# One attention burst per tile, and the state product in a place of its own, in a fused attention, feed-forward and routed-experts kernel

## Chip, core and metric

The kernel runs on one core of a Trainium2 chip. The metric is the device time of one execution in microseconds (us); lower is better. The kernel before took 869.97 to 872.79 us in three timed runs, with a median of 872.28.

## What is computed

Three layers follow each other. The first is a linear-attention recurrence over 768 steps for 4 batches, 8 heads and head size 48; the second a gated feed-forward over the 3072 resulting tokens (width 384, inner width 1536); the third sends each token to one of 8 experts.

```python
# attention, per batch and head
cur = (u * k_t) outer v_t
y_t = r_t @ (state + cur)
state = w[:, None] * state + k_t outer v_t
# feed-forward
x = (silu(x @ w_gate) * (x @ w_val)) @ w_out
# experts: e = argmax(x @ gate); scaled by softmax and a sigmoid gate
out = gate * (relu(x @ w1[e]) @ w2[e])
```

## The kernel before

Attention works on 24 tiles of 128 tokens (NT), one batch each; tile i belongs to batch i % 4 and to the sequence chunk i // 4, of which there are 6 (TPB). Inside a tile the recurrence is written as matrix products. Four kinds of them run on TensorE for a tile:

- the **scores** (`a_scores`, L363): 16 fp32 matmul instructions with 64 rows each, so two of them share the array by rows. They go to banks 6 and 7;
- the **state product** (L378, inside `a_out_mm`): what the state of earlier chunks gives to this tile's output; 8 full-array fp32 instructions;
- the **values** (L387, `a_out_mm`): the masked scores times v; 16 instructions of 48 columns, so two share the array by columns. They add to the state product in the same bank (6);
- the **state matmuls** (L424, `a_state_mm`): k times v, 16 instructions of 48 columns, to bank 7. Tiles of the last chunk (20 to 23) have none.

Around them, VectorE scales k and r by decay tables (`a_scale`, L316), reduces the bonus (L334), copies the scores through a mask into the tile `at` (`a_mask`, L368) and adds the new state (`a_state_up`, L440). GpSimd makes the bonus (L324, L325), a diagonal in `at` (`a_diag`, L343), the scaled keys (`a_keys`, L352) and the decay of the state (`a_decay`, L445). `a_out_ev` takes a tile's output out of PSUM: ScalarE copies a rounded part (L407), VectorE the remainder (L408), first for three column groups into `xT`, then for the fourth into `stage`. After the third tile of a block six DMAs on SP (L412) move `stage` into `xT`. There is one buffer for `krT` (k and r of a tile) and one for `at`.

The feed-forward works on blocks of 3 tiles (BT), 8 blocks (NBLK), 384 tokens each. For each of 12 slices f of the inner width `b_block` issues a gate product (9 matmuls, L475), a down product of slice f - 2 (9 matmuls, L494), a value product (9 matmuls, L475), and `b_act`: Silu on ScalarE (L483), the multiply on VectorE (L484), a rounded cast on ScalarE (L486) and the remainder (L487, on VectorE from block 1 on). Weights and activations are f32r pairs, so a product is three passes over three chunks. Gate and value products go to a ring of banks that `next_gv` hands out: 3, 4 and 5 from block 1 on, 3 and 4 in block 0, where bank 5 is scratch for the weight conversion. Down products gather in banks 0 to 2; ScalarE empties them in slice 1 of the next block (L505).

The order is written out by hand: while block b runs, the attention of the three tiles of block b + 1 is put into 24 slots. Slot 2f comes behind the gate product of slice f, slot 2f + 1 behind its value product and its `b_act`. `a_place` fills them for a tile from slot `first` (0, 8 or 16) on: load, scale, diagonal, then keys, scores and mask, then `a_out` (state product, values, state matmuls, decay, output), the loads of the next tile, and last the state add. For the third tile of a block, scores and `a_out` come one slot earlier (`e`), so behind a gate product. The routing of the block before (`c_units`, two small bf16 products into bank 6), a scan of the weights (L265 on GpSimd) in blocks 2 to 5 and the clearing of a DRAM buffer by 32 DMAs in block 1 have slots too. Block 7 carries no attention; then the experts follow.

Each engine takes its instructions in the order in which they are issued; a wait holds all behind it on that engine.

Of the kernel before, what the change touches and what calls it, by code (L numbers as in the profile page):

```python
# [21 lines left out]
NB, NH, S, HD = 4, 8, 768, 48  # L22
NTOK = NB * S
NT = NTOK // P
TPB = S // P
# [7 lines left out]
BT = 3  # L33
BN = BT * P
# [17 lines left out]
def kernel(  # L52
# [12 lines left out]
    pe, act, dve, pool, sp = nc.tensor, nc.scalar, nc.vector, nc.gpsimd, nc.sync  # L65
# [227 lines left out]
    def a_load_kr(i):  # L293
        n = a_tile(i)
        if i < 3:
            t = kr3[i]
            att[i] = {"k": (t[:, 0], t[:, 2]), "r": t[:, 1]}
            sp.dma_start(out=t[0:HD, 0:2], in_=krT_d[n, 0])
            sp.dma_start(out=t[64 : 64 + HD, 2], in_=krT_d[n, 1, :, 0])
            sp.dma_start(out=t[64 : 64 + HD, 1], in_=krT_d[n, 1, :, 1])  # L300
        else:
            att[i].update({"k": krT[:, 0], "r": krT[:, 1]})
            for j in range(2):
                sp.dma_start(out=krT[64 * j : 64 * j + HD], in_=krT_d[n, j])

    def a_load(i):
        if i < 3:
            rkv = spare[NF - 4 - i][:, 0 : 3 * DM].rearrange("s (a c) -> s a c", a=3)
        else:
            rkv = apool.tile([P, 3, DM], F32, tag="rkv", name="rkv", bufs=2)  # L310
        sp.dma_start(out=rkv, in_=rkv_d[a_tile(i)])
        att.setdefault(i, {}).update({"rn": rkv[:, 0], "kn": rkv[:, 1], "vn": rkv[:, 2]})

    def a_scale(i, parts=(0, 1)):
        if i >= 3:
            dve.tensor_tensor(out=krT, in0=krT, in1=WT, op=ALU.mult)  # L316
        elif 0 in parts:
            dve.tensor_tensor(out=kr3[i][:, 0:2], in0=kr3[i][:, 0:2], in1=WT, op=ALU.mult)
        if i < 3 and 1 in parts:
            dve.tensor_tensor(out=kr3[i][:, 2], in0=kr3[i][:, 2], in1=WkT, op=ALU.mult)  # L320

    def a_bonus(i):
        t = att[i]
        pool.tensor_tensor(out=t["rn"], in0=t["rn"], in1=ub, op=ALU.mult)  # L324
        pool.tensor_tensor(out=t["rn"], in0=t["rn"], in1=t["kn"], op=ALU.mult)  # L325

    def a_diag(i, on_act):
        t = att[i]
        a = apool.tile([P, NH], F32, tag="a", name="a", bufs=2)
        if i < 3:  # L330
            at = spare[NF - 4 - i][:, 3 * DM : 3 * DM + 8 * P].rearrange("s (j p t) -> s j p t", j=2, p=4)
        else:
            at = apool.tile([P, 2, 4, P], F32, tag="at", name="at", bufs=1)
        dve.tensor_reduce(  # L334
            out=a.rearrange("s (j p) -> s p j", j=2), in_=t["rn"].rearrange("s (p j d) -> s p j d", p=4, j=2),
            op=ALU.add, axis=AX.X,
        )
        af = at.rearrange("s j p t -> s (j p) t")
        if on_act:
            for h in range(NH):  # L340
                act.mul(out=af[:, h], in_=ident, mul=a[:, h : h + 1])
        else:
            pool.tensor_tensor(out=af, in0=bc(ident, 1, [P, NH, P]), in1=bc(a, 2, [P, NH, P]), op=ALU.mult)  # L343
        t["at"] = at

    def a_keys(i):
        if i // NB < TPB - 1:
            k = kp
            if i < 3:
                k = kr3[i][:, 0].rearrange("s p t -> s (p t)").rearrange("s (h d) -> s h d", h=NH)  # L350
            att[i]["kp"] = k
            pool.tensor_tensor(  # L352
                out=k[:, :, 0:HD], in0=att[i]["kn"].rearrange("s (h d) -> s h d", h=NH),
                in1=Wk.rearrange("s (h d) -> s h d", h=NH), op=ALU.mult,
            )

    def a_scores(i, b0=6):
        for p in range(4):
            for j in range(2):
                q = slice(64 * j, 64 * j + 64)  # L360
                k, r = att[i]["k"], att[i]["r"]
                k, r = (k[j][:, p], r[:, p]) if i < 3 else (k[q, p], r[q, p])
                pe.matmul(bank[b0 + j][:, p * P : (p + 1) * P], k, r, start=True, stop=True)  # L363

    def a_mask(i, b0=6):
        at = att[i]["at"]
        for j in range(2):
            dve.copy_predicated(  # L368
                at[:, j], bc(mask, 1, [P, 4, P]), bank[b0 + j].rearrange("s (p t) -> s p t", p=4)
            )  # L370

    def a_out_mm(i, b=6, pairs=(3, 0, 1, 2)):
        vn, at, r = att[i]["vn"], att[i]["at"], att[i]["r"]
        c, S0 = i // NB, Sst[i % NB]
        y = bank[b].rearrange("s (p t) -> s p t", p=4)
        if c > 0:
            for p in pairs:
                pe.matmul(  # L378
                    y[:, p], S0[:, p].rearrange("s j e -> s (j e)"), r[:, p, :],
                    start=(p == pairs[0]), stop=False, skip_group_check=True,  # L380
                )
        for p in pairs:
            if i < BT and p < 3:
                pe.matmul(y[:, p], shf[:, p], y3[i], start=True, stop=False)
            for j in range(2):
                h = 2 * p + j
                pe.matmul(  # L387
                    y[64 * j : 64 * j + HD, p], vn[:, h * HD : (h + 1) * HD], at[:, j, p, :],
                    start=(c == 0 and (i >= BT or p == 3)), stop=True, skip_group_check=c > 0,
                )  # L390
            if i < BT and p == 3:
                for j in range(2):
                    q = slice(64 * j, 64 * j + HD)
                    act.copy(out=y3[i][q], in_=y[q, 3])
# [3 lines left out]
    def a_out_ev(i, b=6):  # L398
        y = bank[b].rearrange("s (p t) -> s p t", p=4)
        blk, t = divmod(i, BT)  # L400
        if t == 0:
            xT[blk] = bpool.tile([P, 2, KC, BN], F32R, tag="xT", name="xT", bufs=2)
            if blk > 0:
                stage[blk] = bpool.tile([P, 2, BN], F32R, tag="stage", name="stage", bufs=1)
        o = slice(t * P, (t + 1) * P)
        for x, n in ((xT[blk][:, :, :, o], y[:, 0:KC]),) + (((stage[blk][:, :, o], y[:, KC]),) if blk > 0 else ()):
            act.copy(out=x[:, 0], in_=n)  # L407
            dve.tensor_tensor(out=x[:, 1], in0=n, in1=x[:, 0].bitcast(F32), op=ALU.subtract)  # L408
        if t == BT - 1 and blk > 0:
            for cc in range(KC):  # L410
                for j in range(2):
                    sp.dma_start(  # L412
                        out=xT[blk].bitcast(F32)[64 * j + HD : 64 * j + 64, :, cc, :],
                        in_=stage[blk].bitcast(F32)[64 * j + 16 * cc : 64 * j + 16 * cc + 16],
                    )
# [29 lines left out]
            pool.tensor_tensor(out=sv, in0=sv, in1=bc(pw[:, 0, :, 7], 2, [P, 4, P]), op=ALU.mult)  # L445

    def a_out(i):
        a_out_mm(i)
        a_state_mm(i, 7)
        a_decay(i)  # L450
        a_out_ev(i)

    def a_state(i, b):
        a_state_mm(i, b)
# [2 lines left out]
    hT = {}  # L457
    gvn = [0]

    def next_gv(blk):  # L460
        b = bank[3 + gvn[0] % (3 if blk else 2)]
        gvn[0] += 1
        return b[:, 0:BN]

    PASSES = ((0, 0), (0, 1), (1, 0))

    def b_up(blk, f, *gvs):
        x = xT[blk]
        ps = [next_gv(blk) for _ in gvs]
        first = blk == 0 and f < 2  # L470
        order = [(c, gv, n) for c in range(KC) for gv in range(len(gvs)) for n in range(3)]
        for c, i, n in sorted(order, key=lambda u: first and u[2] == 2):
            wl, xl = PASSES[n]
            o = (gvs[i] * KC + c) * P
            pe.matmul(  # L475
                ps[i], W[f][:, wl, o : o + P], x[:, xl, c, :],
                start=(c == 0 and n == 0), stop=(c == KC - 1 and n == 2),
            )
        return ps
# [112 lines left out]
        return [r1, lambda: c_prefix(st["r"]), r2]  # L592

    def a_place(slots, i, first):
        def load():
            if i + 1 < NT:
                a_load(i + 1)

        def load_kr():
            if i + 1 < NT:  # L600
                a_load_kr(i + 1)

        def bonus():
            if i + 1 < NT:
                a_bonus(i + 1)

        def diag():
            a_diag(i, BT < i < 2 * BT)

        def scores():  # L610
            a_scores(i)
            a_mask(i)

        slots[first].append(load)
        slots[first + (i == BT)].append(lambda: a_scale(i))
        slots[first + 1].append(diag)
        e = 1 if i % BT == BT - 1 else 0
        slots[first + 3 - e] += [lambda: a_keys(i), scores]
        slots[first + 5 - e] += [lambda: a_out(i), load_kr, bonus]
        slots[first + 6].append(lambda: a_state_up(i, 7))  # L620

    raws = {}

# [527 lines left out]
```

## Time and profile before

| | |
|---|---|
| three timed runs | 872.28, 869.97, 872.79 us |
| profiled execution | 870.72 us, its span 869.0 us |
| TensorE busy | 827.0 us, 95% of the span |
| VectorE, ScalarE, GpSimd busy | 460.4, 272.0, 270.5 us |
| gate and value products, L475 | 1728 matmuls, 331.5 us |
| down products, L494 | 864 matmuls, 176.6 us |
| scores, values, state product, state matmuls from SBUF tiles (L363, L387, L378, L424) | 26.3, 22.7, 21.1, 9.0 us |

The span runs from the first to the last instruction; the rest of the execution's time lies around it. Matmuls overlap in the array, so the busy time of a group says less than the distance from the start of one group to the start of the next. That distance is what the text uses for TensorE.

### The profile page before, as it was taken

The numbers are of one execution on the slowest core, as the hardware profiler recorded it, in microseconds if no ns is written. First come the engines' busy times: TensorE is split into PE (matmuls) and PEld (weight loads), VectorE is DVE, ScalarE is ACT, GpSimd is POOL, SyncE is SP. The second block draws the span as 40 slices with busy tenths as digits, with TensorE's granted clock in tenths as the row PEclk, the third lists the DMA queues.
The fourth block names the chain that finished last, engine by engine and source line by source line (L and its number), as shares of the span: only waits on it lengthen the run. The fifth ranks groups of instructions, "written<-read, shape, count | busy, mean of one in ns | idle before, by whom it ended". The sixth has DMA issues, their size and how long they took to land.

```text
span 869.0 us, 13844 instructions
## 1 busy us (share of the span) xinstructions
PE 827.0 (95%) x5427; PEld 797.1 (92%) x5427; DVE 460.4 (53%) x945; ACT 272.0 (31%) x590; POOL 270.5 (31%) x241
## 2 busy tenths in 40 slices
PE   3878889999999999999999999999989999999996
PEld 3667789999999999999999999999989999999996
DVE  7797762454465455465455444234555655565541
ACT  2324342122212211221212221323444444444432
POOL 6655645232344335335245112010110210121022
PEclk9879989999999999999999999999999999999998
DMA  8615426734234322322323211410484443544200
GB/s 256 218 72 192 145 82 153 205 111 123 100 100 131 108 103 68 139 81 95 118 88 129 60 46 47 160 50 1 162 311 148 140 163 113 163 136 166 83 26 35
DMA packets 29769, 104.90 MB, mean 121 GB/s; under 512 B 5175, under 2 KB 14193, under 8 KB 26624
## 3 DMA queue, kind: packets, MB, share of 16 engines
q1 hardware_dynamic: 26368, 94.37, 33.8%
q0 software_dynamic: 3328, 9.56, 2.9%
q8 instruction: 45, 0.74, 0.4%
q14 instruction: 28, 0.23, 0.1%
HBM read 85.84 MB, written 16.41 MB: 118 GB/s over the span
## 4 chain that ended last, share of the span: by engine, by line
PE 83%; DVE 7%; issue 5%; DMA 2%; ACT 1%; POOL 1%; POOLq 0%; SPq 0%; DVEq 0%
PE bank L475 32%; PE bank L494 18%; PE bank L691 11%; PE bank L708 11%; PE bank L363 3%; PE bank L387 3%; PE bank L378 2%; DVE bank L215 2%; DVE bank L214 2%; DMA spare<-in_rkv_dram 2%; DVE cv L216 2%; PE bank L656 1%; PE bank L722 1%; PE bank L424 1%; POOL out_dram L730 0%
## 5 line engine op out<-in xcount | busy, mean ns | idle before, releaser
L475 PE MATMUL bank<-xT,W 128*128 128x384 f32 x1728 | 331.5, 342 | 0.2 <-DVE xT L408 0.2
L475 PEld LDWEIGHTS bank<-xT,W 128*128 128x128 f32 x1728 | 305.0, 189 | 3.2 <-DVE xT L408 0.5
L494 PE MATMUL bank<-W,h 128*128 128x400 f32 x864 | 176.6, 349 | 0.0
L494 PEld LDWEIGHTS bank<-W,h 128*128 128x128 f32 x864 | 156.8, 190 | 1.9 <-issue 0.6
L486 ACT CAST h<-s 128x384 fp32r<-128x384 f32 x96 | 49.2, 512 | 323.5 <-DVE s L484 323.5
L484 DVE TENSOR_TENSOR s<-s,bank 128x384 f32<-128x384 f32 x96 | 53.1, 553 | 174.0 <-PE bank L475 148.6
L708 PE MATMUL bank<-hd,wf 128*128 128x416 f32 (+1 forms) x576 | 113.8, 344 | 0.0
L708 PEld LDWEIGHTS bank<-hd,wf 128*128 128x128 f32 x576 | 104.3, 188 | 0.7 <-DVE hd L695 0.2
L730 POOL DMA_INDIRECT out_dram<-yo,ix x32 | 34.6, 1081 | 206.3 <-DVE yo L726 179.3
L487 DVE TENSOR_TENSOR h<-s,h 128x384 fp32r<-128x384 f32 x84 | 60.5, 720 | 48.6 <-ACT h L486 48.6
L695 DVE SCALAR_TENSOR_TENSOR hd<-bank,hd 128x416 fp32r<-128x416 f32 (+1 forms) x64 | 36.7, 573 | 81.6 <-ACT hd L694 80.1
L343 POOL TENSOR_TENSOR at<-ident,a 128x1024 f32<-128x1024 f32 x19 | 36.2, 1903 | 134.1 <-DVE a L334 134.0
L556 POOL DMA_INDIRECT xs<-rows,slot x24 | 26.2, 1094 | 127.3 <-DVE slot L554 88.7
L640 DVE TENSOR_TENSOR wf<-raw,wf 128x768 fp32r<-128x768 f32 x64 | 61.2, 956 | 7.0 <-ACT wf L639 1.2
L483 ACT ACTIVATE s<-bank 128x384 f32<-128x384 f32 x96 | 47.3, 492 | 49.3 <-PE bank L475 49.3
L691 PE MATMUL bank<-xd1h,wf 128*128 128x416 f32 x192 | 59.3, 367 | 3.5 <-issue 3.5
L694 ACT ACTIVATE hd<-bank 128x416 fp32r<-128x416 f32 (+1 forms) x64 | 32.3, 505 | 87.2 <-PE bank L691 79.4
L639 ACT CAST wf<-raw 128x768 fp32r<-128x768 f32 x64 | 52.8, 825 | 0.0
L691 PE MATMUL bank<-xd0h,wf 128*128 128x416 f32 x144 | 43.8, 362 | 0.0
L691 PEld LDWEIGHTS bank<-xd1h,wf 128*128 128x128 f32 x192 | 36.9, 192 | 4.3 <-issue 3.7
L368 DVE COPY_PREDICATED at<-mask,bank 128x512 f32<-128x512 int32 x42 | 28.3, 728 | 18.0 <-POOL at L343 15.6
L445 POOL TENSOR_TENSOR S<-S,pw 128x512 f32<-128x512 f32 x16 | 17.5, 1095 | 59.7 <-PE bank L378 59.6
(175 smaller groups left out, 948.3 us busy)
## 6 DMA issues: line engine op xcount, KB each, us to landing
raw<-in_w_dram SPq DMA_DIRECT2D x36, 768.0 KB, 4.5
raw<-in_w_dram SPq DMA_DIRECT2D x22, 1152.0 KB, 6.7
rkv<-in_rkv_dram SPq DMA_DIRECT2D x21, 576.0 KB, 5.6
krT<-in_krT_dram SPq DMA_DIRECT2D x42, 192.0 KB, 3.5
xs<-zt SPq DMA_DIRECT2D x32, 197.0 KB, 6.5
xr<-xs SPq DMA_DIRECT2D x6, 591.0 KB, 5.6
spare<-in_w_dram SPq DMA_DIRECT2D x2, 1152.0 KB, 5.2
xT<-stage SPq DMA_DIRECT2D x42, 48.0 KB, 2.1
```

The lines of the kernel that those rows point to most:

```text
L343: pool.tensor_tensor(out=af, in0=bc(ident, 1, [P, NH, P]), in1=bc(a, 2, [P, NH, P]), op=ALU.mult)
L475: pe.matmul(ps[i], W[f][:, wl, o : o + P], x[:, xl, c, :], start=(c == 0 and n == 0), stop=(c == KC - 1 and n == 2),)
L483: act.activation(out=s, in_=g, func=AF.Silu)
L484: dve.tensor_tensor(out=s, in0=s, in1=v, op=ALU.mult)
L486: act.copy(out=h[:, 0], in_=s)
L487: (pool if blk == 0 else dve).tensor_tensor(out=h[:, 1], in0=s, in1=h[:, 0].bitcast(F32), op=ALU.subtract)
L494: pe.matmul(bank[t][:, 0 : DM + 16], h[:, hl, t * P : (t + 1) * P], W[f][:, wl, 2 * KC * P :], start=(f == 0 and n == 0), stop=(f == NF - ...
L639: act.copy(out=wf[:, 0], in_=raw[:, f])
L640: dve.tensor_tensor(out=wf[:, 1], in0=raw[:, f], in1=wf[:, 0].bitcast(F32), op=ALU.subtract)
L691: pe.matmul(ps, wf[:, wl, c * P : (c + 1) * P], xd[xl][:, c, 0:n], start=(i == 0), stop=(i == 3 * KC - 1))
L695: dve.scalar_tensor_tensor(h[:, 1, 0:n], ps, 0.0, h[:, 0, 0:n].bitcast(F32), ALU.max, ALU.subtract)
L708: pe.matmul(bank[c][:, 0:n], wf[:, wl, o : o + P], h[:, hl, 0:n], start=(f == 0 and i == 0), stop=(f == NEF - 1 and i == 2),)
```

## The change

From tile 6 (the first tile of block 2, computed in block 1) on, a tile is issued otherwise; tiles 0 to 5 stay.

- `a_burst(i)`, always in slot `first + 5`, so behind a value product: values of tile i into bank 5, its state matmuls into the bank that `next_gv` gives, the scores of tile i + 1, then the state add and the output.
- `a_next(i + 1)`, one slot later and so behind a gate product: mask of tile i + 1, its state product (`a_past`) into bank 5, its decay. Values of the next burst add to that bank.
- scale, bonus and diagonal are made for the next tile, and krT is reloaded behind the state product. Tile 6 has its first scores and `a_next` in slot 2 of block 1.
- the exception `e` for a block's third tile is gone for these tiles.
- `next_gv` hands out banks 3 and 4 alone, in all blocks.

```diff
+    def a_past(i, b):
+        r, S0 = att[i]["r"], Sst[i % NB]
+        y = bank[b].rearrange("s (p t) -> s p t", p=4)
+        for p in (3, 0, 1, 2):
+            pe.matmul(
+                y[:, p], S0[:, p].rearrange("s j e -> s (j e)"), r[:, p, :],
+                start=(p == 3), stop=False, skip_group_check=True,
+            )
...
-        if c > 0:
-            for p in pairs:
-                pe.matmul(
...
     def a_out(i):
+        if i // NB > 0:
+            a_past(i, 6)
         a_out_mm(i)
         a_state_mm(i, 7)
         a_decay(i)
         a_out_ev(i)
 
+    def a_burst(i):
+        a_out_mm(i, 5)
+        b = next_gv() if i // NB < TPB - 1 else None
+        a_state_mm(i, b)
+        if i + 1 < NT:
+            a_scores(i + 1)
+        a_state_up(i, b)
+        a_out_ev(i, 5)
+
+    def a_next(i):
+        a_mask(i)
+        a_past(i, 5)
+        a_decay(i)
...
-    def next_gv(blk):
-        b = bank[3 + gvn[0] % (3 if blk else 2)]
+    def next_gv():
+        b = 3 + gvn[0] % 2
         gvn[0] += 1
-        return b[:, 0:BN]
+        return b
...
         e = 1 if i % BT == BT - 1 else 0
-        slots[first + 3 - e] += [lambda: a_keys(i), scores]
-        slots[first + 5 - e] += [lambda: a_out(i), load_kr, bonus]
-        slots[first + 6].append(lambda: a_state_up(i, 7))
+        if i + 1 < NT:
+            slots[first].append(lambda: a_load(i + 1))
+        if i < 2 * BT:
...
+            return
+        e = 0
+        if i == 2 * BT:
+            slots[first] += [lambda: a_scale(i), lambda: a_diag(i, False)]
+            slots[first + 2] += [lambda: a_scores(i), lambda: a_next(i), lambda: a_load_kr(i + 1)]
+        slots[first + 3 - e].append(lambda: a_keys(i))
+        if i + 1 < NT:
+            slots[first + 3 - e].append(lambda: a_bonus(i + 1))
+            slots[first + 4 - e].append(lambda: a_scale(i + 1))
+        slots[first + 5 - e].append(lambda: a_burst(i))
+        if i + 1 < NT:
+            slots[first + 5 - e].append(lambda: a_diag(i + 1, False))
+            slots[first + 6 - e].append(lambda: a_next(i + 1))
+        if i + 2 < NT:
+            slots[first + 6 - e].append(lambda: a_load_kr(i + 2))
```

## Rows read from the trace of the kernel before

**Rows 1.** Busy us (x instructions) per engine in block 2; then granted clock, DMA, GB/s:
```profile
209.37:278.19 68.83, 68.83 (x495) 67.02 (x495) 34.69 (x69) 15.47 (x33) 28.28 (x21) 1.00 0.34 111
```

**Rows 2.** Timeline of TensorE around tile 9: start us, us, line, tiles, xcount [idle before]:
```profile
217.36 1.73 PE L475 MATMUL bank<-xT,W 128*128 128x384 f32 x9
219.03 1.16 PE L363 MATMUL bank<-krT 64*128 64x128 f32 x16
220.12 1.84 PE L475 MATMUL bank<-xT,W 128*128 128x384 f32 x9
221.80 1.80 PE L494 MATMUL bank<-W,h 128*128 128x400 f32 x9
223.44 1.75 PE L475 MATMUL bank<-xT,W 128*128 128x384 f32 x9
225.03 1.05 PE L378 MATMUL bank<-krT,S 128*128 128x128 f32 x8
226.01 1.08 PE L387 MATMUL bank<-at,rkv 128*48 128x128 f32 x16
226.92 0.53 PE L424 MATMUL bank<-rkv,kp 128*48 128x48 f32 x16
227.38 1.85 PE L475 MATMUL bank<-xT,W 128*128 128x384 f32 x9
229.07 1.78 PE L494 MATMUL bank<-W,h 128*128 128x400 f32 x9
```

**Rows 3.** Timeline, third and seventh matmul of the eight of a state product:
```profile
199.14 0.39 PE L378 MATMUL bank<-krT,S 128*128 128x128 f32 x2
...
199.59 0.39 PE L378 MATMUL bank<-krT,S 128*128 128x128 f32 x2
```

**Rows 4.** Timeline of block 0: nine down matmuls behind fp32 gate weights (L249):
```profile
94.07 1.88 PE L494 MATMUL bank<-W,h 128*128 128x400 f32 x9
95.78 0.69 PE L475 MATMUL bank<-xT,W 128*128 128x384 f32 x3
```

**Rows 5.** Timeline, slice 1 of block 5: its Silu, and the scores of tile 18:
```profile
424.43 0.50 ACT L483 ACTIVATE s<-bank 128x384 f32<-128x384 f32 x1
...
425.50 1.16 PE L363 MATMUL bank<-krT 64*128 64x128 f32 x16
```

**Rows 6.** Timeline, all engines, behind a value product with attention after it:
```profile
310.75 1.16 PE L363 MATMUL bank<-krT 64*128 64x128 f32 x16
310.92 0.56 DVE L484 TENSOR_TENSOR s<-s,bank 128x384 f32<-128x384 f32 x1 [1.35 <-PE bank L475]
311.29 2.10 POOL L265 TENSOR_TENSOR sc<-raw 128x1152 f32<-128x1152 f32 x1
...
312.06 1.75 DVE L487 TENSOR_TENSOR h<-s,h 128x384 fp32r<-128x384 f32 x1 [0.58 <-ACT h L486]
```

**Rows 7.** Timeline, output of tile 8, then an undisturbed L487 and the state adds:
```profile
201.54 0.56 DVE L408 TENSOR_TENSOR xT<-bank,xT 128x384 fp32r<-128x384 f32 x1 [1.70 <-ACT xT L407]
202.13 0.27 ACT L407 CAST stage<-bank 128x128 fp32r<-128x128 f32 x1 [0.62 <-DVE xT L408]
...
202.43 0.29 DVE L408 TENSOR_TENSOR stage<-bank,stage 128x128 fp32r<-128x128 f32 x1 [0.33 <-ACT stage L407]
...
206.00 0.56 DVE L487 TENSOR_TENSOR h<-s,h 128x384 fp32r<-128x384 f32 x1 [0.58 <-ACT h L486]
...
206.48 0.71 DVE L440 TENSOR_TENSOR S<-bank,S 48x192 f32<-48x192 f32 x2
```

**Rows 8.** Timeline, a tile's diagonal on GpSimd and its mask copy on VectorE:
```profile
194.97 1.92 POOL L343 TENSOR_TENSOR at<-ident,a 128x1024 f32<-128x1024 f32 x1
...
196.92 1.35 DVE L368 COPY_PREDICATED at<-mask,bank 128x512 f32<-128x512 int32 x2 [3.16 <-POOL at L343]
```

**Rows 9.** Timeline of SP at the end of block 6; DMA part, last column us to landing:
```profile
545.76 3.77 SPq L412 DMA_DIRECT2D xT<-stage  x6
...
xT<-stage SPq DMA_DIRECT2D x42, 48.0 KB, 2.1
```

More of the change, by code (lines that the diff above doesn't have):

```diff
@@ L301, in a_load_kr @@
         else:
-            att[i].update({"k": krT[:, 0], "r": krT[:, 1]})
+            att.setdefault(i, {}).update({"k": krT[:, 0], "r": krT[:, 1]})
             for j in range(2):
@@ L370, in a_mask @@
             )
+    def a_past(i, b):
[6 more added lines that the diff above has]
+            )
     def a_out_mm(i, b=6, pairs=(3, 0, 1, 2)):
-        vn, at, r = att[i]["vn"], att[i]["at"], att[i]["r"]
-        c, S0 = i // NB, Sst[i % NB]
+        vn, at = att[i]["vn"], att[i]["at"]
+        c = i // NB
         y = bank[b].rearrange("s (p t) -> s p t", p=4)
-        if c > 0:
-            for p in pairs:
-                pe.matmul(
-                    y[:, p], S0[:, p].rearrange("s j e -> s (j e)"), r[:, p, :],
-                    start=(p == pairs[0]), stop=False, skip_group_check=True,
-                )
         for p in pairs:
@@ L468, in b_up @@
         x = xT[blk]
-        ps = [next_gv(blk) for _ in gvs]
+        ps = [bank[next_gv()][:, 0:BN] for _ in gvs]
         first = blk == 0 and f < 2
@@ L594, in a_place @@
     def a_place(slots, i, first):
[L595 to L616, printed above, removed]
-        e = 1 if i % BT == BT - 1 else 0
-        slots[first + 3 - e] += [lambda: a_keys(i), scores]
-        slots[first + 5 - e] += [lambda: a_out(i), load_kr, bonus]
-        slots[first + 6].append(lambda: a_state_up(i, 7))
+        e = 1 if i % BT == BT - 1 else 0
+        if i + 1 < NT:
+            slots[first].append(lambda: a_load(i + 1))
+        if i < 2 * BT:
+            slots[first + (i == BT)].append(lambda: a_scale(i))
+            slots[first + 1].append(lambda: a_diag(i, BT < i))
+            slots[first + 3 - e] += [lambda: a_keys(i), lambda: a_scores(i), lambda: a_mask(i)]
+            slots[first + 5 - e] += [lambda: a_out(i), lambda: a_load_kr(i + 1), lambda: a_bonus(i + 1)]
+            slots[first + 6].append(lambda: a_state_up(i, 7))
+            return
[13 more added lines that the diff above has]
+            slots[first + 6 - e].append(lambda: a_load_kr(i + 2))
     raws = {}
```

## Prediction

> **What bounds the kernel now.** I read the busy times by stretch first, cut at the first gate product of each block. In a middle block TensorE is busy for the whole of its 68.83 us, at a granted clock of 1.00, while VectorE works for half of it, ScalarE for a quarter and GpSimd for under half [rows 1]. Nothing is waited for there, so a block is worth the sum of the starts on TensorE and nothing else. A change pays in these blocks only if it takes time out of TensorE's own row, and it costs as soon as TensorE waits for anything. Block 0, the last block's attention-free stream and the expert stage aren't rearranged.
>
> Next the timeline of TensorE over one tile, to see what attention costs beside its arithmetic [rows 2]. Start to start, nine plain matmuls of a gate or value product take 1.59 us (223.44 to 225.03) and nine of a down product 1.62 to 1.64. The scores are one visit: the nine in front of it take 1.67 (+0.09), the 16 score instructions 1.09, the nine behind it 1.68 (+0.10). The rest is the second visit: state product 0.98, values 0.91, state matmuls 0.46, and the nine behind 1.69 (+0.10). Together 1.28 + 2.45 = 3.73 us per tile. Of this the arithmetic is less: the state product steps by 0.11 (four steps in 0.45) [rows 3], so eight steps are 0.90, and 0.08 of its 0.98 is the way into the column-tiled values. Eight pairs of scores at the same step would be 0.90, and 0.19 of the 1.09 is start and exit of the row-tiled form. Values behind the state product and state matmuls behind values follow without a jump; both are column tiles.
>
> **The change on TensorE.** It moves, for tiles 6 to 23, values, state matmuls and the next tile's scores into one visit, and makes the state product a visit of its own. No arithmetic is added or removed. The burst is 0.09 (entry, as in front of the scores) + 0.91 + 0.46 + 1.09 + 0.10 (exit) = 2.65 us. The separate state product is 0.90 plus the step back to the f32r products. No such step stands in the trace. The nearest is a full-array fp32 product of the gate weights in front of a down product: the nine behind it take 1.71 against 1.63 [rows 4], so +0.08, and I take 0.98. Sum 3.63 against 3.73: 0.10 saved per tile. It recurs 17 times. The first scores and state product (tile 6, slot 2 of block 1) and the last burst (tile 23, values alone) together cost about what one old tile did. The gain is 17 x 0.10 = **1.7 us**.
>
> Two of these prices have bounds on both sides. The step from column-tiled state matmuls to row-tiled scores isn't in the trace: at best it is free as from values to state matmuls, and 0.2 less is paid (0.1 on each side, as at every other change of tiling in these rows); at worst values entered from f32r are as slow to start as scores (0.10 more). I take the rows as they stand, since each change of tiling in them costs. The step out of the state product lies between nothing and the 0.10 of the other exits. So the gross gain lies between 17 x -0.02 = -0.3 and 17 x 0.38 = 6.5 us.
>
> A rule of the Trainium skill bears on this sum: its page "TensorEngine Tiling (Array Packing)", section Key Properties, says that changing the tiling mode drains TensorE, while changing the tile doesn't. An old tile changes the mode four times (full to row, back, full to column, back), for about 0.7 us beside the arithmetic, a new one three times, and the separate state product none: by that alone 17 x 0.17 = 2.9 us would be saved. The trace agrees on the drains but shows +0.08 where the mode didn't change, from fp32 to f32r [rows 4], so the sum keeps 1.7.
>
> **Banks.** The ring for gate and value products shrinks from three banks to two, and the state matmuls take a bank of it. Products then alternate: a value product needs the multiply (L484) of the slice before, a gate product its Silu. The tightest place is slice 1 of each block, where ScalarE empties the finished block first: there Silu starts at 424.43 and ends at 424.93, and the next gate product, without the scores that stood in front of it, would start at 425.4 [rows 5]. So 0.5 us of cover, cost nothing; with the cover gone it would be paid six times. In a burst the next gate product takes the value product's bank, whose multiply starts 0.17 after the burst's first matmul [rows 6], while the gate product comes at 2.6: covered. The Trainium skill, page "Trainium Kernel Development and Optimization", section Best Practices, says that consistent bubbles can mean SBUF or PSUM ran out; the trace of before shows no bubble in these blocks [rows 1], and the rule would speak against the change only past that 0.5 us.
>
> **The wait that is added.** Values move from bank 6 to bank 5, and the next state product writes bank 5 one gate product after the burst. It must wait until ScalarE and VectorE have taken the tile out (L407, L408). Count from the burst's first matmul, T, by the chain behind a value product [rows 6]: multiply at T + 0.17, the remainder L487 from T + 1.31, and undisturbed it takes 0.56 [rows 7], to 1.87. Now two state adds stand in front of the copies, 0.71 together, to about 2.5; then the first L408 to 3.05, the second L407 behind it, and the second L408 ends at about T + 3.65, all by the steps of [rows 7]. TensorE wants bank 5 at T + 0.91 + 0.46 + 1.09 + 1.69 = T + 4.15. Margin 0.5, cost nothing. Queued behind that wait are the down product and the whole stream, so anything beyond the margin is paid in full.
>
> VectorE then reduces, GpSimd builds the diagonal (1.92) and the mask copy takes 1.35 [rows 8]: from T + 3.65 to about 7.6. The next multiply is wanted at T + 8.6, behind the value product. Covered by 1 us, and by 3 more before its bank is needed. Decay, keys and bonus on GpSimd come later than that and have a slice or more. SP waits for the state product before it reloads krT; behind it stand the next rkv load and, in block 1, the slot-clearing DMAs, all used several slices later.
>
> **The block's end.** The third tile moves from slot 20 to 21, so the copies of stage into xT start nearer to the next block's first gate product. Six issues take 3.77 us, 0.63 apart, and land 2.1 after issue [rows 9]. In blocks 1 to 5 the last lands at T + 3.7 + 3.2 + 2.1 = T + 9.0. The first gate product comes at T + 4.15 + 0.98 + 1.62 + 1.59 = 8.3 and wants the last third 1.06 later and loads weights for it one matmul (0.18) ahead: T + 9.2. Just covered. At the end of block 6 it isn't: tile 23 has no state and no next scores, so T + 0.91 + 0.10 (exit) + 1.69 + 1.63 + 1.59 = 5.9 is the first gate product, while the copies (without the state adds) start at T + 3.0. Its second third wants weights at 6.3 and its copy lands at 3.0 + 1.9 + 2.1 = 7.0, a wait of 0.7; the last third wants them at 7.5 and lands at 8.3, 0.8 more. So TensorE loses **1.5 us** once.
>
> **Sum.** -1.7 + 1.5 = -0.2 us. The profiled execution took 870.72 us, 1.56 under the median of the three timed runs (872.28); the mean of the four is 871.4. I forecast 871.2 us, no change that can be seen: about 0.3% (2.6 us) is what a measurement of this kernel can tell from none.
>
> **Rivals.** (a) *The switch is cheap.* If scores behind state matmuls start without a drain and the state product leaves without one, 17 x 0.38 = 6.5 us go and 1.5 come back: 866.4. For it: values to state matmuls cost nothing. Against it: the jump at every other change of form. From 0.24 per tile on (4.1 less 1.5, 868.8) it is faster by 0.3%. (b) *Bank 5 comes late; slower.* The place is the wait of the separate state product. L487 took 1.75 instead of 0.56 where GpSimd ran its scan product (L265) beside it [rows 6]. In the burst that puts the second L408 at T + 4.85 and costs 0.7 us per tile; it decides once GpSimd's long products overlap T + 1.3. Blocks 2 to 5 have two scans each that GpSimd takes ahead of the diagonal: 8 x 0.7 = 5.6, so 876.8. Against it: these scans hang on loads that SP issues behind the krT reload, so they should have run some slices before the burst. (c) *The end of the block is early enough.* If the copies land sooner than 2.1 us, the 1.5 shrinks and 870 remains: within my case. (d) *The visits don't merge*, the instructions between them keeping a product apart: 871.4, the same verdict.
>
> **Chances.** Forecast with (c) and (d), 0.60; (a), in whole or from that point on, 0.21; (b), or a bank of the ring that comes late, 0.19. Faster by over 0.3%: 0.21; within 0.3%: 0.60; slower: 0.19. The range takes in (a) and most of (b): 866 to 876.5; the likeliest case alone is 869 to 873.
>
> **What would show it.** In the timeline of TensorE, after a value product: L387, L424, L363, then nine L475 of about 1.69; one gate product later L378 with no idle in front of it and then nine L494 of about 1.71. A middle block of 68.5 us instead of 68.83. Idle on TensorE in front of the last block's first gate product, about 1.5 us in two pieces, released by the copies of stage. The prediction is wrong if L378 waits for L408, if a product waits for L483 or L484, or if L363 follows L424 without the 0.1 us jump.

## The result, and the profile after

The changed kernel took 861.56, 863.15, 861.66 and 861.61 us, median 861.63; the kernel before took 871.57 in the same measurement. The ratio is 0.989, interval 0.987 to 0.991. I had forecast 871.2 and a range down to 866.0: the prediction is wrong. The profiled execution took 861.56 us, its span 859.8, which is 9.2 us under the span before.

Where the 9.2 us lie can be read from the windows cut at each block's first gate product. Columns: window, its length, then busy us (x instructions) of TensorE, its weight loads, VectorE, ScalarE, GpSimd, the granted clock, DMA share, GB/s. First the kernel before (its block 2 is [rows 1]):

```profile
35.51:140.54 105.03, 88.82 (x623) 82.29 (x620) 76.77 (x144) 38.45 (x94) 61.03 (x56) 0.92 0.37 129
140.54:209.37 68.83, 68.83 (x496) 67.03 (x496) 30.05 (x66) 15.58 (x33) 22.62 (x19) 1.00 0.56 152
...
347.02:415.85 68.83, 68.83 (x496) 67.03 (x496) 35.85 (x70) 15.48 (x33) 28.24 (x21) 1.00 0.33 108
...
484.31:552.02 67.71, 67.71 (x448) 65.52 (x447) 28.99 (x62) 15.57 (x33) 12.85 (x10) 1.00 0.18 47
552.02:614.14 62.12, 62.12 (x355) 61.40 (x354) 22.72 (x54) 17.76 (x36) 3.40 (x6) 1.00 0.17 65
614.14:869.00 254.86, 243.70 (x1435) 237.21 (x1434) 134.54 (x289) 112.34 (x233) 37.51 (x35) 0.98 0.42 140
```

Then the changed kernel, block 0, 1, 2, 4, 6, 7 and the experts:

```profile
34.19:137.69 103.50, 90.22 (x623) 83.17 (x620) 76.80 (x144) 38.46 (x94) 61.03 (x56) 0.90 0.38 133
137.69:208.11 70.42, 70.42 (x520) 68.60 (x519) 32.51 (x70) 15.38 (x33) 25.78 (x22) 1.00 0.54 149
208.11:276.34 68.23, 68.23 (x496) 66.74 (x496) 34.73 (x69) 15.37 (x33) 27.48 (x21) 1.00 0.33 110
...
344.56:413.50 68.94, 68.54 (x495) 66.69 (x495) 35.79 (x70) 15.38 (x33) 27.60 (x21) 1.00 0.34 109
...
481.38:546.55 65.17, 65.17 (x423) 63.29 (x423) 26.47 (x58) 15.38 (x33) 10.81 (x9) 1.00 0.15 43
546.55:610.16 63.61, 62.71 (x355) 61.38 (x355) 22.71 (x54) 17.76 (x36) 3.37 (x6) 1.00 0.20 69
610.16:859.80 249.64, 242.09 (x1435) 236.01 (x1434) 134.42 (x289) 112.34 (x233) 37.96 (x35) 1.00 0.42 143
```

Three parts:

| stretch | before | after | difference |
|---|---|---|---|
| up to block 1, code not changed | 140.54 | 137.69 | -2.85 |
| blocks 1 to 7, where the change is | 473.60 | 472.47 | -1.13 |
| experts, code not changed | 254.86 | 249.64 | -5.22 |

Within blocks 1 to 7: block 1 +1.59 (tile 6 has its first scores and state product there as an extra), blocks 2, 3 and 5 -0.60 each, block 4 +0.11, block 6 -2.54, block 7 +1.49. So the blocks that carry the change give 1.1 us, and seven eighths of the difference between the two profiles lie where nothing was edited.

The new stream, one tile of block 2 on TensorE (start us, us, line, tiles, xcount), answers [rows 2]; L494 is now the gate and value product, L513 the down product, L390 the values, L427 the state matmuls, L363 the scores, L376 the state product:

```profile
220.89 1.75 PE L494 MATMUL bank<-xT,W 128*128 128x384 f32 x9
222.57 1.08 PE L390 MATMUL bank<-at,rkv 128*48 128x128 f32 x16
223.48 0.53 PE L427 MATMUL bank<-rkv,kp 128*48 128x48 f32 x16
223.94 1.16 PE L363 MATMUL bank<-krT 64*128 64x128 f32 x16
225.03 1.84 PE L494 MATMUL bank<-xT,W 128*128 128x384 f32 x9
226.71 1.05 PE L376 MATMUL bank<-krT,S 128*128 128x128 f32 x8
227.52 1.88 PE L513 MATMUL bank<-W,h 128*128 128x400 f32 x9
229.23 3.31 PE L494 MATMUL bank<-xT,W 128*128 128x384 f32 x18
```

Start to start: 0.91, 0.46, 1.09 and nine of 1.68, the prices of the prediction. The state product takes 0.81 up to the down product's start, and the nine of that 1.71.

The output chain of the same tile on VectorE and ScalarE (the steps of [rows 7]):

```profile
223.88 0.56 DVE L506 TENSOR_TENSOR h<-s,h 128x384 fp32r<-128x384 f32 x1 [0.58 <-ACT h L505]
224.35 0.72 DVE L443 TENSOR_TENSOR S<-bank,S 48x192 f32<-48x192 f32 x2
225.10 0.56 DVE L411 TENSOR_TENSOR xT<-bank,xT 128x384 fp32r<-128x384 f32 x1
225.69 0.27 ACT L410 CAST stage<-bank 128x128 fp32r<-128x128 f32 x1 [1.47 <-DVE xT L411]
225.99 0.29 DVE L411 TENSOR_TENSOR stage<-bank,stage 128x128 fp32r<-128x128 f32 x1 [0.33 <-ACT stage L410]
```

Bank 5 is free at 226.28, 3.71 behind the burst's first matmul (222.57), and the state product wants it at 226.71, 4.14 behind. No idle stands in front of L376 in any block.

The two block ends that wait, on TensorE and on SP. At the start of block 7, then at the start of block 4:

```profile
543.63 3.78 SPq L415 DMA_DIRECT2D xT<-stage  x6
...
547.78 0.47 PEld L494 LDWEIGHTS bank<-xT,W 128*128 128x128 f32 x3 [0.78 <-DMA xT<-stage]
...
548.99 0.47 PEld L494 LDWEIGHTS bank<-xT,W 128*128 128x128 f32 x3 [0.73 <-DMA xT<-stage]
```

```profile
340.07 4.57 SPq L415 DMA_DIRECT2D xT<-stage  x6
...
346.21 0.48 PEld L494 LDWEIGHTS bank<-xT,W 128*128 128x128 f32 x3 [0.72 <-DMA xT<-stage]
```

The experts. Before, TensorE stands still once, right behind the branch into the experts (L938, a comparison with the flag that says how full the experts are), and then works at a granted clock of 0.50 (1.2 of 2.4 GHz) for 3.4 us:

```profile
638.91 0.71 PE L691 MATMUL bank<-xd1h,wf 128*128 128x416 f32 x1 [3.51 <-issue]
```

```profile
638.40:641.80 3.40, 2.89 (x8) 2.79 (x9) 0.00 (x0) 0.00 (x0) 0.00 (x0) 0.50 1.00 384
```

After, the same product (L708) follows without a break and at full clock:

```profile
631.26 0.35 PE L708 MATMUL bank<-xd1h,wf 128*128 128x416 f32 x1
```

The trace records the branch itself: 4.77 us on TensorE before, 0.88 after. ("issue" means that TensorE waited for no engine and no transfer that the profile shows.) It is the same instruction of the same code, so the question of all that follows is what made it shorter.

### The profile page after: what moved, and what is told of

The parts are those of the page before. It is cut to its first block, busy times and chain, and to the rows that moved or that the text cites. A ratio compares the mean times of both kernels' runs of the same rounds, so it can differ in the third digit from the quotient of the medians.

```text
span 859.8 us, 13873 instructions
## 1 busy us (share of the span) xinstructions
PE 821.9 (96%) x5427; PEld 792.9 (92%) x5427; DVE 459.8 (53%) x945; ACT 271.2 (32%) x590; POOL 267.9 (31%) x241
## 4 chain that ended last, share of the span: by engine, by line
PE 84%; DVE 8%; DMA 2%; issue 2%; ACT 1%; SPq 1%; POOL 0%; POOLq 0%; DVEq 0%; ACTq 0%
PE bank L494 31%; PE bank L513 17%; PE bank L708 12%; PE bank L725 12%; PE bank L363 3%; PE bank L390 2%; PE bank L376 2%; DVE bank L215 2%; DVE bank L214 2%; DMA spare<-in_rkv_dram 2%; DVE cv L216 2%; PE bank L673 1%; PE bank L739 1%; SPq L415 1%; DVE krT L316 1%
## 5 line engine op out<-in xcount | busy, mean ns | idle before, releaser
L494 PE MATMUL bank<-xT,W 128*128 128x384 f32 x1728 | 331.4, 342 | 1.5 <-DMA xT<-stage 1.3
L494 PEld LDWEIGHTS bank<-xT,W 128*128 128x128 f32 x1728 | 305.1, 189 | 5.8 <-DMA xT<-stage 2.2
L513 PE MATMUL bank<-W,h 128*128 128x400 f32 x864 | 176.0, 348 | 0.0
L513 PEld LDWEIGHTS bank<-W,h 128*128 128x128 f32 x864 | 155.9, 189 | 0.5 <-issue 0.2
L506 DVE TENSOR_TENSOR h<-s,h 128x384 fp32r<-128x384 f32 x84 | 51.8, 616 | 48.7 <-ACT h L505 48.7
L575 POOL DMA_INDIRECT xs<-rows,slot x24 | 23.8, 991 | 112.8 <-DVE slot L573 51.5
L708 PE MATMUL bank<-xd1h,wf 128*128 128x416 f32 x192 | 58.2, 361 | 0.0
L708 PE MATMUL bank<-xd0h,wf 128*128 128x416 f32 x144 | 43.8, 362 | 0.0
L708 PEld LDWEIGHTS bank<-xd1h,wf 128*128 128x128 f32 x192 | 36.0, 188 | 0.5
L324 POOL TENSOR_TENSOR rkv<-rkv,ub 128x384 f32<-128x384 f32 x21 | 21.8, 1037 | 46.3 <-DMA rkv<-in_rkv_dram 46.3
```

Of the source, the lines that this page charges most:

```text
L494: pe.matmul(ps[i], W[f][:, wl, o : o + P], x[:, xl, c, :], start=(c == 0 and n == 0), stop=(c == KC - 1 and n == 2),)
L506: (pool if blk == 0 else dve).tensor_tensor(out=h[:, 1], in0=s, in1=h[:, 0].bitcast(F32), op=ALU.subtract)
L513: pe.matmul(bank[t][:, 0 : DM + 16], h[:, hl, t * P : (t + 1) * P], W[f][:, wl, 2 * KC * P :], start=(f == 0 and n == 0), stop=(f == NF - ...
L708: pe.matmul(ps, wf[:, wl, c * P : (c + 1) * P], xd[xl][:, c, 0:n], start=(i == 0), stop=(i == 3 * KC - 1))
```

## The experiments

**First question: did the attention edit make the branch shorter, or did something that any edit does?** TensorE's instructions come by a queue of their own, in pieces of 16,384 bytes, 45 in this kernel for 10,952 recorded instructions. In the profile before, such a fetch starts at 636.3, behind the start of the branch (634.0); after, one starts at 628.1, ahead of it (630.0). The edit adds 20 instructions (waits) to TensorE's stream ahead of the branch. So the theory: where the branch stands against these fetches decides. "Place" below is the branch's number among TensorE's recorded instructions in the order of their starts, modulo 256: 180 before, 200 after. In every kernel 16 weight loads and products from ahead of the branch start after it, so places compare with each other. The rival: the new order of attention leaves engines or queues in another state, and this shortens the experts.

The dummies that shift the place are one-column products into a bank that nobody reads, put into block 7; each is two instructions on TensorE:

```diff
+                slots[8].append(lambda: [
+                    pe.matmul(bank[7][:, 0:1], ones, ones[:, 0:1], start=True, stop=True) for _ in range(10)
+                ])
```

`b_again` and `a_again` are the two kernels unchanged; `b_pad10` is the kernel before with ten dummies (place 200), `a_pad118` the changed kernel with 118 (its branch is number 8392 + 236 = 8628, which is 8372 + 256, so place 180 again).

> The kernel before, unchanged, for a second trace. Its first trace and that of the changed kernel differ by 9.2 us of span: 1.1 in the seven blocks that the change touches or follows (blocks 1 to 7), 5.2 in the expert stage and 2.9 ahead of block 1, where the code is the same. Theory 1 (instruction fetch): TensorE's branch into the expert stage stands, counted in TensorE's instructions, just ahead of the fetch of the next piece of its program, so it waits for it: L938 takes about 4.8 us again on TensorE, 871 us in all. Theory 2 (chance): the 4.8 us and the half-clock stretch behind it belong to one execution; here the branch takes 0.9 to 5 and the time scatters by 5 us between runs. Ahead of block 1 both expect the stretches of half clock to lie elsewhere and the start of block 1 to move by up to 3 us.

> The changed kernel once more. Theory 1: its branch on TensorE stands 20 instructions later than before and meets a fetch that is already done: about 0.9 us again, 861.6 us. Theory 2: between 0.9 and 5 us, and times from 861 to 867.

> The kernel before with ten one-column matmuls (20 TensorE instructions) more in slot 8 of block 7, into an unused column of bank 7: the branch now stands where it stands in the changed kernel, modulo the 256 instructions of one fetch. They cost about 0.04 us each, 0.5 in all. Theory 1: the branch takes about 0.9 us, no half-clock stretch behind it, the expert stage 249.6 instead of 254.9, the whole about 866.8. Theory 2 or any theory in which attention's order shortens the expert stage: 872, the branch as in the kernel before.

> The changed kernel with 118 such matmuls (236 instructions): the branch stands where it stands in the kernel before, modulo 256. They cost some 4.7 us in block 7. Theory 1: the branch takes 4 to 5 us again with a half-clock stretch behind it, the expert stage about 254.9, the whole 861.6 + 4.7 + 5.2 = 871.5. Theory 2: 866.3.

Measured against 870.76 for the kernel before: `b_again` 870.28 (ratio 0.9986, interval 0.9967 to 1.0005), `a_again` 862.47 (0.9896, 0.9866 to 0.9926), `b_pad10` 861.52 (0.9902, 0.9871 to 0.9932), `a_pad118` 873.24 (1.0026, 1.0005 to 1.0046). Ten products that do nothing give the kernel before the whole gain. 118 of them take it from the changed kernel: its block 7 is 66.65 us instead of 63.60, so 3.05 us are theirs, and 870.2 is left. The branch took 6.52, 0.74, 0.54 and 6.04 us. The rival is out: attention is the same within each pair. The size is only in part explained: by the branch alone I had expected 866.8 us for `b_pad10`. Its profile (span 859.4) is 9.6 us under the first one of the kernel before; 5.1 of that lie in the experts, 4.8 ahead of block 1 (135.7 against 140.5 us), and its block 7 is 0.35 longer.

**Second question: what about the place?** In the source, a hint that names the branch stands some slices ahead of it; perhaps its distance counts. `b_hint0` moves that line and nothing else:

```diff
+            (0, 1): [lambda: tc.mark_branch_hint_location("size", hint=LIKELY, engines=ENGINES)],
-            (4, 1): [lambda: tc.mark_branch_hint_location("size", hint=LIKELY, engines=ENGINES)],
```

`b_pad64` has 64 dummies (place 52). `b_ring2` gives the kernel before the two-bank ring, to price that part of the change alone; it has 12 waits less, so place 168.

```diff
-        b = bank[3 + gvn[0] % (3 if blk else 2)]
+        b = bank[3 + gvn[0] % 2]
```

> The kernel before with one line moved: the place that names the likely branch into the expert stage (the hint) stands in slice 0 of the first expert pass instead of slice 4. No matmul is added; the branch stands where it stood (180 modulo 256). Theory 1a: the next piece of TensorE's program, with the branch's target, is asked for only when a fetch starts between the hint and the branch; before, none does in the last 175 instructions. With the hint earlier one does: the branch takes under 1 us, 861 to 862 us. Theory 1b: only the branch's own place counts: 4.8 to 6.5 us at the branch, 870.8.

> The kernel before with 64 one-column matmuls (128 instructions, some 1.7 us by the 3.05 us that 118 of them cost), branch at 52 modulo 256, hint some 175 ahead at 133. Theory 1a: a fetch (seen at 154 to 236 modulo 256 all along the stream) falls between hint and branch: under 1 us, 861.5 + 1.4 = 863. Theory 1b: with the branch a long way in front of the next fetch, 4.8 to 6.5 us: 872.

> The kernel before with the ring of banks 3 and 4 alone for gate and value products in all blocks, attention as before. The reading by rows: no product waits, blocks 2 to 4 stay at 68.83 us. It has 12 TensorE waits less ahead of the branch, which moves to 168 modulo 256 with no fetch between hint and branch: 4.8 to 6.5 us there as before, 870.8 in all. If the two banks were what made the changed kernel faster: 862.

Against 870.2: `b_hint0` 871.09 (1.0008, 0.9992 to 1.0024), branch 5.92 us. This says nothing about the hint. In the traces of the kernel before and of `b_hint0` alike, TensorE's only hint ahead of the branch is recorded 0.9 us into the program, and the next one right behind the branch. Moving the line moved nothing that the trace shows, so `b_hint0` is one more run of the kernel before, and theories 1a and 1b are not told apart by it. `b_pad64` 865.43 (0.9934, 0.9914 to 0.9954), branch 0.38, and its block 7 is 63.81 instead of 62.12, so 1.7 us are the dummies'; its six runs spread from 861.94 (the profiled one) to 867.45. `b_ring2` 862.64 (0.9905, 0.9872 to 0.9939): I had expected it to stay long and was wrong about place 168, where the branch took 0.39. Its blocks say what I wanted of the ring: 68.83 us in blocks 1 to 4, as before. The third bank was worth nothing.

`b_ring2` left a doubt, since the ring itself could have shortened the branch. So the ring with six dummies (place 180 again) and with three (174), and the kernel before with four (188):

> The kernel before with a ring of two banks, and six one-column matmuls in block 7 (0.2 us). With the ring alone the branch into the experts was 168 instructions past a multiple of 256 on TensorE and took 0.39 us; with the six it is at 180, where it took 4.8 to 6.5 us in four programs. Theory (the place decides): the branch takes 5 to 6 us again, the tail grows from 249.6 to 255 to 257 us, the time is 870 to 871.5 us. Rival (the ring itself, its 12 fewer waits or the earlier end of something, made that run fast): the branch stays under 1 us, the time at 862.8.

> The same with three one-column matmuls, so the branch stands at 174. Places 168 and 200 were fast, 180 slow. If the slow places are a stretch that begins between 168 and 180, this run narrows its start: about 862.7 us with a branch under 1 us, or 870 to 871.5 us with one of 5 to 6. If the branch is neither (2 to 4 us), the place shifts the cost by degrees. I hold the slow end for a little likelier.

> The kernel before with four one-column matmuls in block 7 (0.15 us): the branch stands at 188. Place 180 was slow, 200 fast. Theory (a fetch of TensorE's program that starts only behind the branch makes it slow, and starts ahead of it from some place between 180 and 200 on): one of 870.5 us with a branch of 4.5 to 6.5 us, or 862 us with one under 1 us; it narrows the end of the slow stretch. A branch under 1 us with a fetch that starts behind it would speak against the fetch as the cause.

Against 871.08: `r2_pad6` 871.50 (1.0003, 0.9985 to 1.0020), `r2_pad3` 863.77 (0.9904, 0.9869 to 0.9939), `b_pad4` 867.40 (0.9958, 0.9939 to 0.9977). Three dummies more, and the same kernel is 7.7 us longer. I had held the long end for likelier at 174, and it was the short one; at 188 I had expected one end or the other, and the cost is in between. In the timeline of TensorE, the first expert product behind the branch in `r2_pad6`, `r2_pad3` and `b_pad4`:

```profile
638.60 0.71 PE L691 MATMUL bank<-xd1h,wf 128*128 128x416 f32 x1 [5.06 <-issue]
```

```profile
635.29 0.35 PE L691 MATMUL bank<-xd1h,wf 128*128 128x416 f32 x1
```

```profile
635.32 0.53 PE L691 MATMUL bank<-xd1h,wf 128*128 128x416 f32 x1 [2.65 <-issue]
```

The thirteen profiles of kernels that take this branch, by place; the branch's duration and the start of the nearest fetch of TensorE's instructions, counted from the branch's start, are from the trace's records of that instruction and that queue; "experts" is the stretch from the last block's end to the end of the span:

| place | kernel | branch us | fetch starts | experts us | median us |
|---|---|---|---|---|---|
| 168 | `b_ring2` | 0.39 | none until +4.0 | 249.62 | 862.64 |
| 174 | `r2_pad3` | 0.39 | none until +3.5 | 249.73 | 863.77 |
| 180 | before | 4.77 | +2.3 | 254.86 | 871.57 |
| 180 | `b_again` | 6.52 | +4.1 | 257.08 | 870.28 |
| 180 | `b_hint0` | 5.92 | +3.4 | 256.58 | 871.09 |
| 180 | `r2_pad6` | 6.32 | +3.9 | 256.91 | 871.50 |
| 180 | `a_pad118` | 6.04 | +3.6 | 255.86 | 873.24 |
| 188 | `b_pad4` | 3.92 | +1.5 | 253.90 | 867.40 |
| 200 | after | 0.88 | -1.9 | 249.63 | 861.63 |
| 200 | `a_again` | 0.74 | -1.7 | 249.66 | 862.47 |
| 200 | `b_pad10` | 0.54 | -2.0 | 249.72 | 861.52 |
| 200 | `a_e23` (below) | 0.64 | -1.8 | 249.52 | 859.84 |
| 52 | `b_pad64` | 0.38 | -5.4 | 249.57 | 865.43 |

In the six long branches the branch ends 2.4 to 2.5 us behind the start of a fetch that starts after it. At 200 the fetch is already under way, and the branch ends 2.5 to 2.8 us behind its start. At 52 it is long done, and at 168 and 174 TensorE starts 40 to 46 recorded instructions behind the branch (16 of them from ahead of it) before it fetches at all: what follows the branch was there. So the cost of the branch is the wait for one fetch that was begun too late. At place 180 the experts are 5.2 to 7.4 us longer in the profiles than at 200, while the medians differ by 8 to 10. The rest isn't explained: the time ahead of block 1 varies from 135.4 to 140.6 us over these profiles, and not by place (138.4 in `r2_pad6`, 140.4 in `r2_pad3`).

The Trainium skill says this on its page "Runtime: NRT & Kernel Launch", section Instruction fetch mechanics: instructions are fetched ahead in order, in blocks of 16 KiB or 256 instructions, and a taken branch whose target isn't in the fetched window has to wait for a fetch. The runs agree: 16,384 bytes each, and a like price at 8372 (4.77 to 6.52 us) and at 8628 (6.04), 256 apart. The price here is 3.5 to 6.1 us over the 0.4 of an undisturbed branch. The experts grow by another 0.6 to 1.4 us, which goes with the stretch at a granted clock of 0.50 behind the stop: 0.6 to 0.9 us where it lasts 3.4 us (before, `a_pad118`, `b_pad4`), 1.3 to 1.4 where it lasts 6.8. The seven short branches have no such stretch.

The traces hold a second branch of TensorE near the end of the experts (L1086 in the kernel before), 2573 recorded instructions after the first. It takes 2.5 to 3.8 us in the kernels at 174 and 180, and 0.35 to 0.65 in the others. It costs nothing: the span ends 7.73 us behind its start in all thirteen. So a late fetch is paid for only where what comes next waits for TensorE.

**Third question: the wait at the start of block 7.** My 1.5 us there was a sum of rows. If it is the stage copies alone, the last burst one slot earlier removes it. The first try kept the old exception `e` for every third tile:

```diff
-        e = 0
+        e = 1 if i % BT == BT - 1 else 0
```

> The changed kernel with the old exception for a block's third tile kept: its burst one slot earlier, behind a gate product. The branch stands as in the changed kernel (200 modulo 256). The waits for the copies of stage at the start of a block go: block 6 to 7 1.5 us, block 4 about 0.4 to 0.7. By that 862.0 - 2.0 = 860. If the place behind the value product is worth something on TensorE, blocks 2 and 3 grow above 68.23.

This took 16,695 us. Its blocks 2 to 4 took 71.8 us, and then the general path for unusual data ran, and the stretch behind block 7 took 16,070 us. By the code, a burst behind a gate product takes one of the two banks, so that the value product is handed the bank of the gate product before Silu has read it: the kernel computes other activations. The general path, which computes everything anew, is taken, among other cases, when an expert gets more than 512 tokens; that other activations sent it there fits, but no run shows it. That the burst must stand behind both up products, where it has state matmuls, is thus by the code a condition of the two-bank ring and no choice. Blocks 2 to 4 grew for another reason: the scores in the earlier burst waited 2.0 us for VectorE's scaling of the next tile (L316), and in block 2, for one, the granted clock then was 0.5 for 3.4 us. One thing it still shows: its block 7, whose stage copies start a slot earlier, took 62.13 us. Tile 23 has no state matmuls and takes no bank, so it alone can be moved:

```diff
-        e = 0
+        e = 1 if i == NT - 1 else 0
```

> The changed kernel with its last burst (tile 23, which has no state matmuls and so takes no bank of the ring) one slot earlier, behind the gate product of slice 10 of block 6. Theory: the 1.48 us that block 7 grew (63.60 us against 62.12) is TensorE waiting for the copies of stage into xT, and nothing else. The copies then start some 3.3 us earlier, so block 7 falls to 62.1 us, block 6 stays at 65.2 and the tail at 249.6: about 1.5 us less than the changed kernel, 860.1 to 861.0 us. Rival: the wait is that of another engine or of the loads behind it; then block 7 stays at 63.6.

It took 859.84 us against 871.08 (0.987, 0.984 to 0.990; five executions took 858.33 to 862.57, and the sixth, at a mean granted clock of 0.56, took 1343.2, for which I have no profile). Block 7 is 62.12 us, block 6 65.15: all of the 1.49 is back, and this is the fastest version of the case. The issues of the copies, and the next block's products without a wait:

```profile
540.00 4.92 SPq L415 DMA_DIRECT2D xT<-stage  x6
...
544.69 3.31 PE L494 MATMUL bank<-xT,W 128*128 128x384 f32 x18
```

## Why the prediction was wrong

**The step that failed** is one sentence: block 0 and the expert stage "aren't rearranged". From that I let them keep their time. The expert stage lost 5.2 us because the branch into it moved by 20 instructions. The edit did that, but so do ten idle products, so it says nothing about attention. The row was there in the trace before: 3.51 us of TensorE idle, put down to "issue". I had the window of the experts too (TensorE busy for 243.70 of 254.86 us, granted clock 0.98), and took them as a constant. A rival "the branch becomes cheaper (or dearer)" with a price of 3 to 4 us was to be had from that row. None of the prediction's own signs of being wrong appeared: it failed outside the stretches that it watched.

**The head, -2.85 us, is not the change.** Over the thirteen profiles block 0 starts at 31.9 to 35.5 us and takes 103.5 to 105.1, so block 1 starts at 135.4 to 140.6. Six of them are of kernels whose code there is that of before, and these span the whole range. The stretches of half clock fall elsewhere from profile to profile, but they don't explain it: block 0 has a granted clock of 0.92 before, where it is longer, and 0.90 after. The cause stays open. It adds some 5 us of spread to any single profile.

**The sum for blocks 1 to 7** was -0.2 and is -1.1, in three terms, of which two were wrong and in part cancel:

- *The tile: -0.10, measured -0.20.* Blocks 2, 3 and 5 lose 0.60 us for three tiles. The burst came as priced: 0.91, 0.46, 1.09 and 0.09 on each side. The mis-sized term is the exit of the separate state product. I had eight steps of 0.11, 0.90, and 0.08 on top, from the nine down products behind fp32 gate weights [rows 4]. The nine behind L376 do take 1.71, but L376 hands over after 0.81, not 0.90: its last step is short by what the first of the nine is long. The 0.08 was counted twice. So the exit costs nothing, 0.89 in all, and 17 tiles give 3.4 us. The Trainium skill's page "TensorEngine Tiling (Array Packing)", section Key Properties, asks for a drain only where the tiling mode changes; on this exit the trace agrees with it (0.81 + 1.71 against 0.90 + 1.63). The prediction's 2.9 us by that rule rests on 0.7 us beside an old tile's arithmetic; its own terms add up to 0.56 (0.09 + 0.19 + 0.10 + 0.08 + 0.10), so the estimate by it would be 17 x 0.14 = 2.4 us, still nearer the 3.4 than my 1.7. Its remark that values follow the state product without a jump contradicts its own 0.08 on that step; the sum used the 0.08.
- *The start of block 7: +1.5, measured +1.49*, in the two pieces forecast (0.7 and 0.8; 0.78 and 0.73).
- *The ends of blocks 1 to 5: 0, measured 0.7 at one of five.* I had 0.2 us of margin. At the start of block 4 SP's six issues took 4.57 us instead of 3.77, and the last third of the gate product came 0.72 late.

With these, -3.4 + 1.5 + 0.7 = -1.2, against -1.13 read.

The second counting could have been seen in the trace of before. The six L249 products in front of the nine of [rows 4] take 0.59 us up to the start of the nine (94.07), some 0.08 less than six steps of 0.11:

```profile
93.48 0.73 PE L249 MATMUL bank<-G,gt 128*128 128x16 f32 x6
```

**What was right:** bank 5 is free at T + 3.71 (forecast T + 3.65) and wanted at T + 4.14 (4.15), so rival (b) didn't occur. The ring of two banks costs nothing, by `b_ring2` too. Rivals (c) and (d) didn't occur: the block's end costs what was forecast, and the visits merge. Rival (a) was half right: the state product leaves freely, but scores behind state matmuls still take 1.09, so they start as they did behind f32r products.

So about the edit the forecast "no change that can be seen" holds: at place 200, 861.63 and 862.47 with it, 861.52 without (0.35 of that the dummies'); at place 180, 870.2 with it after taking off the dummies, 870.2 to 871.6 without. About the kernel it was wrong: what the change gains here is the branch's new place, which ten idle products give as well.

## To carry to other kernels

Where TensorE takes a branch, an edit that adds or removes instructions anywhere ahead of it also moves the branch against the instruction fetches; compare two orders only at an equal place, or read the branch's duration in both traces before crediting the edit. An idle of TensorE marked "issue" behind a branch is a few us that a handful of idle instructions can give back, if what follows waits for TensorE. In a sum of starts, take a group's length up to the next group's start and not steps times count, or its exit is paid twice.

## What the runs showed of the hardware

- A branch on TensorE takes 0.38 to 0.39 us where no fetch is waited for (places 52, 168 and 174), and 3.9 to 6.5 where the fetch starts after the branch. Six instructions (174 to 180) make the difference, and the price falls again over 188 (3.9) to 200 (0.5 to 0.9).
- The late fetch starts 1.5 to 4.1 us behind the branch, and other transfers keep the DMA engines busy meanwhile (DMA share 1.00 around 638 us in the kernel before). The share is as high around the short branch (1.01 from 626 to 638 us in the changed kernel), so it alone doesn't make the branch long. Whether the fetch queues behind those transfers wasn't tried.
- Full-array fp32 products hand over to f32r products at no cost (0.89 us for eight, 0.81 up to the next start), while changes between row-tiled, column-tiled and full products cost about 0.1 us on each side.
